# Sixteen projection units as whole 128-row products into one PSUM bank, rounded straight from PSUM, and a first pair of rows loaded on an earlier schedule

## The chip, the cores and the metric

The kernel runs on one core of a Trainium2 chip. The time is the device time of one execution in microseconds (us). Below, PE is TensorE, ACT is ScalarE, DVE is VectorE, POOL is GpSimd, and SP is the engine that issues nearly all DMAs. PEld is the profile's name for PE's weight loads.

## What is computed

A gate mixes an attention layer and a Fourier mixing layer, both on the same x of 2048 rows by 512 columns:

```python
qkv = (x @ wqkv) -> q, k, v, 32 heads of 16      # S = 2048, D = 512
a = softmax(q k^T / 4) v @ wo
b = dft_seq_re @ (x @ dft_hid_re^T) - dft_seq_im @ (x @ dft_hid_im^T)
g = sigmoid((x * gate_w).sum(-1))
out = g * a + (1 - g) * b
```

## The kernel before

**Number format.** Most matrix products run on fp32 values rounded to TensorE's float32r format. Each operand is kept as two parts, a rounded one (`hi`) and what is left of it (`lo`, rounded too), and one product is summed from three: hi·hi, lo·hi and hi·lo. `split` (line 351) makes the parts: ACT copies into float32r (line 352), and DVE or POOL subtracts (line 353).

**Halves.** `halves_of` (line 200, product at 204) cuts each 128-row contraction into two products of 64 rows. They lie in the upper and the lower half of the array and write to two PSUM banks, so that the result is the sum of the two banks. The scans, which run between other products later on, also use rows 0 to 47 and 64 to 111.

**Units and slots.** `project_t` (line 480) makes one unit of the q and k projections: 128 columns of the weights against 512 rows of x, over four blocks `d` of the contraction and three part products each, so twelve steps. A step is called a slot here. `products` (line 343) issues them and calls `beside` (line 307) after each. `beside` counts the slots and runs what is due: `after(n, f, ...)` (line 282) registers a piece of work for n slots later. So the order of every engine's instructions follows from slot numbers, while the times on the chip follow from the waits. Engines work through their own instructions strictly in that order.

**The end of a unit before.** ACT copies bank 0 to `tx` (line 489). Five slots later DVE adds bank 1 (line 492). Nine slots after the unit ACT rounds the sum to `hi` (tile `eh`, three buffers), then POOL subtracts to `lo` (tile `el`, four buffers). The two parts go to DRAM (`q_d`, `k_d`) by DMAs due 14 and 20 slots after the unit (line 499). Work registered by `after` carries line 297 in the profile. An `eh` buffer is written again three units later, so the store of three units before has to have landed.

**The first sixteen units.** They run before any scan (`pace[0]` is None). Here they are called u0 to u15: u0 (q), u1 (k) and u2 (q) take x block c=0; u3 and u4 take c=1, u5 and u6 c=2, u7 and u8 c=3 (q then k each time); u9 to u15 are further q units. Between u7 and u8 stand the gate sums (line 573), 16 plain fp32 products of 128 rows by 32 columns, and in the middle of u8 four transposes of their result. u0, u2, u4 and u6 write to the `s1` banks, all others to the two `wide` tiles in turn, named `xy`. x is split while this goes on (line 567): the four blocks `d` of x block c are split at slots 24c-6+4d, ACT and DVE doing one instruction each.

**The rows of the first pair.** The scans search the maxima of the scores, and need rows of q and k of two heads in SBUF. `load_scan_beside` (line 299) reads those of the first pair from `q_d` and `k_d` with eight DMAs on SP (line 116), four for each head; it is due 22 slots after u8, and the eight are 7 slots apart. 84 slots after u8, at the end of u15, `scan_at(PACE)` starts the scans: one every 3.9 slots, each with a product for either head (line 154) and a maximum on DVE (line 156). The first one stands behind the third slot of u16.

**SP.** SP issues its DMAs in order. They share eight semaphores in turn, so a DMA is only issued when the one eight before it has landed; a wait on `DMAHW0` to `DMAHW7` in the order's rows is such a wait, or one for data.

Of the kernel before, what the change touches and what calls it, by code (L numbers as in the profile page):

```python
# [10 lines left out]
F32 = mybir.dt.float32  # L11
F32R = mybir.dt.float32r
# [6 lines left out]
P = 128  # L19
# [6 lines left out]
ND = D // P  # L26
# [40 lines left out]
def build(tc, xT, wqkv, wo, wrT, wiT, cr, ci, ct, gate, out):  # L67
    nc = tc.nc
    with ExitStack() as ctx:
# [130 lines left out]
        def halves_of(ps, lhs, rhs, first, last):  # L200

            for j in range(2):
                r = slice(64 * j, 64 * j + 64)
                nc.tensor.matmul(ps[j], lhs[r], rhs[r], start=first, stop=last)  # L204
# [6 lines left out]
        def wide(i, name):  # L211
            return psf.tile([P, 2, 512], F32, tag=f"wide{i}", name=name)
# [56 lines left out]
        pace = [None, 0.0]  # L269
        with ExitStack() as pf:  # L270
# [6 lines left out]
            def xy():  # L277
                turns[0] += 1
                ps = wide(turns[0] % 2, "xy")
                return ps[:, 0, :], ps[:, 1, :]  # L280

            def after(n, f, *args):

                count[0] += 1
                due.append((slots[0] + n, count[0], f, args))
# [13 lines left out]
            def load_scan_beside(p):  # L299
                scanned[p], loads = row_loads(p, nc.sync, kf_d if p else k_d)  # L300
                for n, load in enumerate(loads):
                    after(7 * n, load)

            def scan_at(spacing):
                pace[0] = spacing
# [34 lines left out]
                    scan_folded(n, 1, *beds)  # L340
                    return n

            def products(ps, parts):
                n = 0
                for lhs, rhs in parts:
                    for a, b in ((0, 0), (0, 1), (1, 0)):
                        halves_of(ps, lhs[a], rhs[b], n == 0, n == 3 * len(parts) - 1)
                        n += 1
                        beside()

# [15 lines left out]
            for ph, plain, pair in ((0, range(NB - 2), (NB - 2, NB - 1)), (1, range(2, NB), (0, 1))):  # L366
                split_up = [(ph, t, u) for half in range(2) for t in pair for u in (2 * half, 2 * half + 1)]
                whole = [(ph, t, u) for t in plain for u in range(NU)]
# [29 lines left out]
            with ExitStack() as px:  # L398
                wb = px.enter_context(tc.tile_pool(name="wb", bufs=1))
                ep = px.enter_context(tc.tile_pool(name="ep", bufs=2))  # L400
# [78 lines left out]

                def project_t(w, dst, f, c, ps=None):  # L480
                    ps = ps or xy()
                    products(ps, [([w[i][d][:, f * P:(f + 1) * P] for i in range(2)], xs[d, c])
                                  for d in range(ND)])
                    tx = ep.tile([P, 512], F32, tag="tx", name="tx", bufs=1)
                    folded = dst is k_d
                    s = ep.tile([P, 512], F32, tag="ty", name="s", bufs=3)
                    hi = ep.tile([P, 512], F32R, tag="eh", name="eh", bufs=3)
                    lo = ep.tile([P, 512], F32R, tag="el", name="el", bufs=4)
                    nc.scalar.copy(tx, ps[0])
                    on_vector = pace[0] in (None, SUMS)  # L490
                    if on_vector:
                        after(5, nc.vector.tensor_add, s, ps[1], tx)
                    else:
                        after(3, nc.scalar.copy, s, ps[1])
                        after(5, nc.gpsimd.tensor_add, s, s, tx)
                    late = 0 if on_vector else 6

                    def store(i, v):
                        nc.sync.dma_start(dst[f][:, i, c * 512:(c + 1) * 512], v.bitcast(F32))
                        if folded and f and c % 2:  # L500
                            nc.sync.dma_start(kf_d[f][:, i, c * 512:(c + 1) * 512], v.bitcast(F32))

                    if folded and f == 1:
                        difference(f, c, s)
                    if folded and f == 2:
                        after(10, nc.sync.dma_start, ks_d[f][:, c * 512:(c + 1) * 512], s)
                    after(9 + late, nc.scalar.copy, hi, s)
                    after(10 + late + late // 3, nc.gpsimd.tensor_sub, lo, s, hi.bitcast(F32))
                    after(14 + late, store, 0, hi)
                    after(20 + late, store, 1, lo)  # L510
# [73 lines left out]
                for n, (w, dst, f, c) in enumerate(order):  # L584
                    lead = s1() if n in (0, 2, 4, 6) else None
                    project_t(w, dst, f, c, lead and (lead[:, 0, :], lead[:, 1, :]))
                    if n == 7:
                        gate_sums()
                after(22, load_scan_beside, 0)
                after(84, scan_at, PACE)  # L590
                for f, c in [(2, 0), (3, 0)] + [(f, c) for f in range(1, ND) for c in range(1, NC)]:
                    project_t(wq, q_d, f, c)
# [59 lines left out]
            with ExitStack() as py:  # L652
# [36 lines left out]
                for n, (ph, t, u) in enumerate(coef):  # L689
# [12 lines left out]
                    hi, lo = ready.pop(n)  # L702
# [47 lines left out]
        with ExitStack() as pa:  # L750
# [143 lines left out]
            parts = []  # L894
# [299 lines left out]
            for step in range(NP * PERIODS):  # L1194
                p, i = step // PERIODS, step % PERIODS
# [133 lines left out]
```

## Time and profile before

| | |
|---|---|
| time, median of 3 runs | 1715.07 us (1714.08 to 1715.12) |
| the profiled execution | 1715.43 us, its span 1713.6 us |
| granted TensorE clock | 0.999 |
| instructions | 36496 |
| HBM read, written | 158.34 MB, 81.01 MB |

The profile is of one execution. Times in it count from the span's start; the 1.8 us between span and time lie around the program. A row of the timeline gives the start in us, the length in us, engine, line, operation, tiles, how many instructions were merged into it, and in brackets how long the engine was idle before it and what ended that. Matmul records are longer than the time that a product takes up, since products overlap in the array: what counts is the distance between starts.

### The profile page before, as it was taken

What the parts mean: (1) busy time and instruction counts of PE and PEld (TensorE: products, weight loads), DVE (VectorE), ACT (ScalarE), POOL (GpSimd) and SP (SyncE); (2) the same over time, 40 slices, a digit from 0 to 9 for tenths busy, and PEclk for the clock granted to TensorE, in tenths of its full rate; (3) what the DMA queues carried; (4) which work ended last, traced back from release to release, by engine and by line L of the source; (5) the groups of instructions that cost most, each with busy time, mean ns of one, the idle gap of its engine ahead of it and who ended that gap; (6) DMA issues with size and microseconds to landing.
All of it is one profiled execution on the core that took longest, in us unless ns stands there. A gap on an engine that the chain in (4) does not pass through costs nothing.

```text
span 1713.6 us, 36496 instructions
## 1 busy us (share of the span) xinstructions
PE 1700.1 (99%) x13560; PEld 1033.2 (60%) x13560; DVE 1189.9 (69%) x2179; ACT 1496.6 (87%) x2472; POOL 764.1 (45%) x909
## 2 busy tenths in 40 slices
PE   9999999999999999999999999999999999999998
PEld 6888888989888895333333333333345555555554
DVE  5798888889899996666666676666642455654343
ACT  6447889888888888999999999999998988888876
POOL 3583335755555762433535455353422333334222
PEclk9999999999999999999999999999999999999999
DMA  7783457533337665356544445453436465576733
GB/s 255 237 286 86 149 153 224 155 107 108 112 106 199 176 132 109 89 128 149 138 112 113 121 114 135 100 124 85 95 73 144 133 148 148 141 160 168 192 93 126
DMA packets 148962, 240.97 MB, mean 141 GB/s; under 512 B 50048, under 2 KB 60784, under 8 KB 142192
## 3 DMA queue, kind: packets, MB, share of 16 engines
q1 hardware_dynamic: 133520, 217.27, 47.5%
q0 software_dynamic: 14688, 20.33, 5.0%
q8 instruction: 106, 1.74, 0.5%
q10 hardware_dynamic: 576, 1.05, 0.2%
q14 instruction: 72, 0.59, 0.1%
HBM read 158.34 MB, written 81.01 MB: 140 GB/s over the span
## 4 chain that ended last, share of the span: by engine, by line
PE 95%; issue 1%; POOL 1%; DMA 1%; DVE 1%; ACT 0%; SPq 0%; DVEq 0%; POOLq 0%; ACTq 0%
PE pvb L775 29%; PE xy L204 24%; PE s L229 19%; PE s L173 9%; PE s L204 9%; PE s L154 5%; POOL el L297 1%; DMA raws<-wqkv 0%; DMA qs<-q_d 0%; DVE y L890 0%; DVE fold L179 0%; ACT fold L177 0%; DVE s L297 0%; SPq L543 0%; SPq L542 0%
## 5 line engine op out<-in xcount | busy, mean ns | idle before, releaser
L253 ACT ACTIVATE eb<-s 128x1024 f32<-128x1024 f32 x512 | 582.0, 1137 | 59.6 <-PE s L229 59.5
L261 ACT ACTIVATE e<-s 128x512 f32<-128x512 f32 x1022 | 612.3, 715 | 0.0
L156 DVE TENSOR_REDUCE mx<-s 128x2 f32<-128x1024 f32 x380 | 461.0, 1224 | 197.5 <-PE s L154 197.3
L775 PE MATMUL pvb<-eb,va 128*17 128x512 f32 x2052 | 514.6, 597 | 0.0
L775 PE MATMUL pvb<-e,va 128*17 128x512 f32 x2044 | 513.6, 597 | 0.0
L179 DVE CUSTOM_DVE_ANT_0 fold<-s,fold 128x512 f32<-128x512 f32 x644 | 433.2, 690 | 57.3 <-PE s L173 29.9
L177 ACT ACTIVATE fold<-s 128x512 f32<-128x512 f32 x644 | 381.4, 603 | 76.8 <-PE s L173 58.9
L229 PEld LDWEIGHTS s<-qs,ks 50*128 50x128 f32 x2048 | 215.4, 185 | 361.4 <-ACT eb L253 269.4
L229 PE MATMUL s<-qs,ks 50*128 50x512 f32 x2048 | 424.3, 435 | 0.0
L204 PE MATMUL xy<-b,c 64*128 64x512 f32 x2448 | 394.7, 392 | 0.2 <-ACT c L352 0.2
L173 PE MATMUL s<-ks,qs 48*128 48x512 f32 x1288 | 306.1, 403 | 1.7 <-DVE mx L179 0.9
L204 PEld LDWEIGHTS xy<-b,c 64*128 64x128 f32 x2448 | 285.7, 187 | 16.9 <-issue 1.0
L173 PEld LDWEIGHTS s<-ks,qs 48*128 48x128 f32 x1288 | 167.1, 184 | 40.4 <-DVE mx L179 10.7
L775 PEld LDWEIGHTS pvb<-eb,va 128*17 128x17 f32 x2052 | 70.0, 96 | 188.1 <-issue 178.5
L154 PE MATMUL s<-ks,qs 48*128 48x512 f32 x760 | 158.5, 394 | 0.9 <-DMA qs<-q_d 0.9
L204 PE MATMUL s<-b,b 64*128 64x512 f32 x1050 | 136.3, 391 | 0.0
L794 POOL DMA_DIRECT2D r_d<-lc x31 | 18.0, 580 | 260.6 <-DVE lc L793 212.9
L204 PE MATMUL xy<-w,b 64*128 64x512 f32 x768 | 114.8, 392 | 0.0
L204 PEld LDWEIGHTS s<-b,b 64*128 64x128 f32 x1050 | 100.3, 185 | 23.4 <-issue 1.0
L787 POOL DMA_DIRECT2D lc<-ob x124 | 63.0, 515 | 114.4 <-DVE ob L784 109.6
L384 POOL TENSOR_TENSOR c<-craw,c 128x512 fp32r<-128x512 f32 x84 | 110.2, 1312 | 6.7
L796 POOL DMA_DIRECT2D rb<-r_d x124 | 60.5, 494 | 110.6 <-DMA r_d<-lc 104.7
(148 smaller groups left out, 1567.3 us busy)
## 6 DMA issues: line engine op xcount, KB each, us to landing
qs<-q_d SPq DMA_DIRECT2D x68, 256.0 KB
craw<-cr SPq DMA_DIRECT2D x60, 256.0 KB
craw<-ct SPq DMA_DIRECT2D x48, 256.0 KB
ks<-k_d SPq DMA_DIRECT2D x46, 256.0 KB
kept_None<-sum SPq DMA_DIRECT2D x40, 256.0 KB
craw<-kept_None SPq DMA_DIRECT2D x40, 256.0 KB
qs<-q_d SPq DMA_DIRECT2D x68, 128.0 KB
craw<-ci SPq DMA_DIRECT2D x32, 256.0 KB
```

Of the source, the lines that this page charges most:

```text
L154: nc.tensor.matmul(ps[:, j, :], qs[b:b + 48, qb * P:(qb + 1) * P], ks[b:b + 48, c * 512:(c + 1) * 512], start=True, stop=True)
L156: nc.vector.tensor_reduce(mx[p][:, :, qb, c], ps, axis=AX.X, op=ALU.max)
L173: nc.tensor.matmul(ps, qs[b:b + 48, qb * P:(qb + 1) * P], ks[b:b + 48, c * 512:(c + 1) * 512], start=True, stop=True)
L177: nc.scalar.activation(fold[j], ps, AF.Relu)
L179: nc.vector.tensor_tensor_reduce(out=fold[j], in0=ps, in1=fold[j], scale=1.0, scalar=-3.0e38, op0=ALU.add, op1=ALU.max, accum_out=mx[p][:, ...
L204: nc.tensor.matmul(ps[j], lhs[r], rhs[r], start=first, stop=last)
L229: nc.tensor.matmul(pss[j], ks[b:b + 50, kb * P:(kb + 1) * P], qs[b:b + 50, q0:q0 + 512], start=True, stop=True)
L253: nc.scalar.activation(e, ps, AF.Exp, scale=SCALE)
L261: nc.scalar.activation(e[j], pss[j], AF.Exp, scale=SCALE)
L384: sub(lo, raw, hi.bitcast(F32))
L775: nc.tensor.matmul(pvb[r:r + VC, :], va[:, kb, 2 * p + j, :], es[c][j], start=kb == 0, stop=kb == NB - 1, tile_position=(0, r))
L787: nc.gpsimd.dma_start(lc[32 * n:32 * n + 32, :], ob[r + DH:r + VC, :].rearrange("p (s e) -> p s e", e=16))
```

## The change

Three things change, all in the first 60 us of the program.

1. In the first sixteen units `products` issues one product of 128 rows into one bank in place of the two of 64 rows. That is 192 products and weight loads in place of 384.
2. At the end of such a unit ACT rounds the bank straight to `hi`, as the unit's last product ends. Four slots later DVE subtracts `hi` from the bank to give `lo`. The stores are due 5 and 9 slots after the unit. The copy to `tx`, the addition, and POOL's subtraction are gone for these units.
3. The first pair's eight loads are due from 14 slots after u8, 6 slots apart.

```diff
             def load_scan_beside(p):
                 scanned[p], loads = row_loads(p, nc.sync, kf_d if p else k_d)
                 for n, load in enumerate(loads):
-                    after(7 * n, load)
+                    after((7 if p else 6) * n, load)
...
-            def products(ps, parts):
+            def products(ps, parts, whole=False):
                 n = 0
                 for lhs, rhs in parts:
                     for a, b in ((0, 0), (0, 1), (1, 0)):
-                        halves_of(ps, lhs[a], rhs[b], n == 0, n == 3 * len(parts) - 1)
+                        if whole:
+                            nc.tensor.matmul(ps[0], lhs[a], rhs[b], start=n == 0, stop=n == 3 * len(parts) - 1)
+                        else:
+                            halves_of(ps, lhs[a], rhs[b], n == 0, n == 3 * len(parts) - 1)
                         n += 1
                         beside()
...
                 def project_t(w, dst, f, c, ps=None):
                     ps = ps or xy()
+                    whole = pace[0] is None
                     products(ps, [([w[i][d][:, f * P:(f + 1) * P] for i in range(2)], xs[d, c])
-                                  for d in range(ND)])
+                                  for d in range(ND)], whole)
+                    if whole:
+                        hi = ep.tile([P, 512], F32R, tag="eh", name="eh", bufs=3)
+                        lo = ep.tile([P, 512], F32R, tag="el", name="el", bufs=4)
+                        nc.scalar.copy(hi, ps[0])
+                        after(4, nc.vector.tensor_sub, lo, ps[0], hi.bitcast(F32))
+                        for i, (wait, v) in enumerate(((5, hi), (9, lo))):
+                            after(wait, nc.sync.dma_start, dst[f][:, i, c * 512:(c + 1) * 512], v.bitcast(F32))
+                        return
...
-                after(22, load_scan_beside, 0)
+                after(14, load_scan_beside, 0)
```

In the rows below the numbers at the ends of names tell buffers apart, and the brackets name the semaphores that an instruction waits for. In the new program's rows the lines are those of the new file.

ACT, before, from u3's copy to u5's. `tx_463`, `tx_502` and `tx_541` are u3, u4 and u5; `eh_465` is u3's `hi`; `b20_223` and `b22_225` are the hi parts of x block c=2, d=2 and d=3.

```order
L489 COPY tx_463<-xy_425 128x512 [waits PE_49,Activation_49]
L352 CAST b20_223<-raws_243 128x512 [waits DMAHW0_49]
L352 CAST b22_225<-raws_244 128x512 [waits DMAHW1_49]
L297 CAST eh_465<-s_464 128x512 [waits DMAHW1_49,DVE_49]
L489 COPY tx_502<-s1_468 128x512 [waits PE_49,Activation_49]
L352 CAST b24_227<-raws_241 128x512 [waits DMAHW2_49]
L297 CAST eh_504<-s_503 128x512 [waits DMAHW3_49,DVE_49]
L352 CAST b26_229<-raws_242 128x512
L489 COPY tx_541<-xy_507 128x512 [waits PE_49,Activation_49]
```

The same stretch of ACT in the new program; `eh_405`, `eh_428` and `eh_451` are the `hi` of u3, u4 and u5.

```order
L491 CAST eh_405<-xy_381 128x512 [waits DMAHW1_49,DVE_49,PE_49]
L355 CAST b20_223<-raws_243 128x512 [waits DMAHW0_49]
L355 CAST b22_225<-raws_244 128x512
L491 CAST eh_428<-s1_408 128x512 [waits DVE_49,DMAHW3_49,PE_49,Activation_49]
L355 CAST b24_227<-raws_241 128x512 [waits DMAHW2_49]
L355 CAST b26_229<-raws_242 128x512
L491 CAST eh_451<-xy_431 128x512 [waits DMAHW5_49,DVE_49,PE_49]
```

u3's rounding, which waits for the landing of u0's `hi` store (`DMAHW1`), stood behind the splits of x block c=2, d=2 and d=3; now it stands ahead of them.

DVE, new program, the same stretch: the splits' `lo` parts and the units' `el`.

```order
L356 TENSOR_TENSOR b21_224<-raws_243,b20_223 128x512 [waits DMAHW0_49,Activation_49]
L297 TENSOR_TENSOR el_406<-xy_381,eh_405 128x512
L356 TENSOR_TENSOR b23_226<-raws_244,b22_225 128x512 [waits DMAHW1_49,Activation_49]
L297 TENSOR_TENSOR el_429<-s1_408,eh_428 128x512 [waits DMAHW2_49,Activation_49]
L356 TENSOR_TENSOR b25_228<-raws_241,b24_227 128x512 [waits Activation_49]
```

The places are those of before; what stood there was the addition of the two banks, and is now the subtraction that gives `lo`.

SP, before, from the second store of u10 to the last of the first pair's loads; `eh_798` and `el_799` are u11's stores, `eh_836` and `el_837` u12's.

```order
L499 DMA q_d3_80<-el_760 128x512 [waits Pool_49]
L116 DMA ks_750<-k_d0_81 32x1x2048 [waits DMAHW3_49]
L499 DMA q_d1_78<-eh_798 128x512 [waits DMAHW4_49,Activation_49]
L499 DMA q_d1_78<-el_799 128x512 [waits DMAHW5_49,Pool_49]
L116 DMA qs_749<-q_d0_77 32x2048 [waits DMAHW6_49]
L499 DMA q_d1_78<-eh_836 128x512 [waits DMAHW7_49,Activation_49]
L116 DMA ks_750<-k_d0_81 16x2048 [waits DMAHW0_49]
L499 DMA q_d1_78<-el_837 128x512 [waits DMAHW1_49,Pool_49]
L116 DMA qs_749<-q_d0_77 16x2048 [waits DMAHW2_49]
```

The same stretch of SP in the new program, with u11's `eh_611` and `el_612` and u12's `eh_634`.

```order
L297 DMA q_d3_80<-el_589 128x512 [waits DVE_49]
L116 DMA ks_570<-k_d0_81 32x1x2048 [waits DMAHW3_49]
L297 DMA q_d1_78<-eh_611 128x512 [waits DMAHW4_49,Activation_49]
L116 DMA qs_569<-q_d0_77 32x2048 [waits DMAHW5_49]
L297 DMA q_d1_78<-el_612 128x512 [waits DMAHW6_49,DVE_49]
L116 DMA ks_570<-k_d0_81 16x2048 [waits DMAHW7_49]
L297 DMA q_d1_78<-eh_634 128x512 [waits DMAHW0_49,Activation_49]
L116 DMA qs_569<-q_d0_77 16x2048 [waits DMAHW1_49]
```

Each of the last three loads moved past one store. The first five keep their places among the stores, and the last now stands behind u12's `hi` store instead of its `lo` store.

DVE, new program, where the scans begin: `el_677` and `el_696` are u14 and u15, `mx_706` takes the scans' maxima.

```order
L297 TENSOR_TENSOR el_677<-xy_660,eh_676 128x512 [waits DMAHW2_49,Activation_49]
L156 TENSOR_REDUCE mx_706<-s1_705 128x2 [waits PE_49]
L297 TENSOR_TENSOR el_696<-xy_679,eh_695 128x512 [waits DMAHW6_49,Activation_49]
L156 TENSOR_REDUCE mx_706<-s1_720 128x2 [waits PE_49]
L156 TENSOR_REDUCE mx_706<-s1_733 128x2 [waits PE_49]
```

u15's subtraction stands between the first two maxima. Before, u15's banks were summed on POOL, and no other DVE work stood between the first maxima.

## The prediction

> **What bounds the kernel now.** I read the page's busy times and chain first, then the timeline of the first 62 us engine by engine, since the change touches nothing later.
>
> ```profile
> PE 1700.1 (99%) x13560; PEld 1033.2 (60%) x13560; DVE 1189.9 (69%) x2179; ACT 1496.6 (87%) x2472; POOL 764.1 (45%) x909
> PE 95%; issue 1%; POOL 1%; DMA 1%; DVE 1%; ACT 0%; SPq 0%; DVEq 0%; POOLq 0%; ACTq 0%
> ```
>
> PE's own work is 95% of the chain that ends last, and PE runs in a fixed order. So the change is worth what it moves the point at which the scans run, and PE carries that shift to the end. I take the product of the first scan's second half, at 58.80 here, as that point. PE's timeline up to it:
>
> ```profile
> 21.61 2.68 PEld L204 LDWEIGHTS xy<-b,w 64*128 64x128 f32 x24
> 21.83 2.88 PE L204 MATMUL xy<-b,w 64*128 64x512 f32 x24
> 24.55 2.88 PE L204 MATMUL s<-b,c 64*128 64x512 f32 x24
> 29.87 0.30 PEld L204 LDWEIGHTS xy<-b,w 64*128 64x128 f32 x4 [0.56 <-DVE b L353]
> 29.87 0.73 PE L204 MATMUL xy<-b,w 64*128 64x512 f32 x4
> 34.10 1.66 PE L204 MATMUL xy<-b,c 64*128 64x512 f32 x12
> 35.70 0.42 PEld L297 LDWEIGHTS s<-ident,zr 128*128 128x128 f32 x4 [0.37 <-issue]
> 35.70 0.66 PE L297 MATMUL s<-ident,zr 128*128 128x128 f32 x4
> 36.28 1.64 PE L204 MATMUL xy<-b,c 64*128 64x512 f32 x12
> 37.76 19.88 PE L204 MATMUL xy<-b,w 64*128 64x512 f32 x174
> 57.48 0.40 PE L154 MATMUL s<-ks,qs 48*128 48x512 f32 x1
> 58.77 0.18 PEld L154 LDWEIGHTS s<-ks,qs 48*128 48x128 f32 x1 [1.33 <-DMA ks<-k_d]
> 58.80 0.46 PE L154 MATMUL s<-ks,qs 48*128 48x512 f32 x1 [0.92 <-DMA qs<-q_d]
> ```
>
> Rows two and three are u5 and u6. They start 2.72 us apart, which for 12 slots is 0.2267 us a slot. Of these 2.72 us the weight loader is busy for 2.68. The two rows at 29.87 are the eleventh and twelfth slot of u7, after a wait for a split. u8 begins at 34.10, with the gate sums ahead of it and four transposes in its middle; the long row begins with u9. The last three show the scan's first half at 57.48 and its second half waiting for rows until 58.80, 1.3 us.
>
> **The whole product's pace.** No row shows a float32r product of 128 rows by 512 columns, so I bound it. It has half the weight loads, so the loader no longer binds (12 x 2.68/24 = 1.34 us a unit), if loads still run under products. In u5's rows they do: 2.68 us of loads lie within 2.72 us, and each half of the array is also streaming. The streaming is measured by the gate sums:
>
> ```profile
> 31.42 0.13 PEld L573 LDWEIGHTS s<-raws,gw 128*32 128x32 f32 x4 [0.30 <-issue]
> 31.85 0.13 PEld L573 LDWEIGHTS s<-raws,gw 128*32 128x32 f32 x4 [0.30 <-issue]
> L573 PE MATMUL s<-raws,gw 128*32 128x512 f32 x32 | 3.6, 595 | 0.0
> L204 PE MATMUL xy<-b,w 64*128 64x512 f32 x336 | 42.4, 389 | 0.1
> ```
>
> Their groups of four records, side by side, start 0.43 us apart, and one is 0.595 long, so 0.165 us of a record is tail. A half product's record of 0.389 less this tail is 0.22 us. **I take 0.22 us a slot.** The program has 16 gate products and the trace 32 records, so each fp32 product passes twice; if each pass also reads its 512 columns twice, a single pass takes 0.214, the lower end. The upper end is load and product in turn, 0.22 + 0.112 (2.68/24) = 0.332.
>
> [...]
>
> **What becomes late first.** With `hi` rounded at a unit's end, its buffer is needed 9 slots sooner. The stores cannot land sooner, because they queue behind the loads of x and the weights:
>
> ```profile
> 12.90 0.62 ACT L297 CAST eh<-s 128x512 fp32r<-128x512 f32 x1 [0.24 <-DVE s L297]
> 15.22 0.34 SPq L554 DMA_DIRECT2D ones_d<-ones  x1
> 15.87 0.34 SPq L499 DMA_DIRECT2D q_d<-eh  x1
> 20.08 1.14 ACT L352 CAST b<-raws 128x512 fp32r<-128x512 f32 x2
> 23.53 0.62 ACT L297 CAST eh<-s 128x512 fp32r<-128x512 f32 x1 [2.31 <-DMA q_d<-eh]
> 25.47 0.62 ACT L297 CAST eh<-s 128x512 fp32r<-128x512 f32 x1 [0.31 <-DVE s L297]
> 22.23 0.68 DVE L353 TENSOR_TENSOR b<-raws,b 128x512 fp32r<-128x512 f32 x1
> ```
>
> u0's `hi` store is issued at 15.87, and u3's rounding waits for its landing until 23.53. u0's `hi` is ready at 13.52 already; the store only comes to its turn on SP behind `ones_d`, whose data were there from the start. An earlier `hi` doesn't move it, so 23.53 stands. But before, the casts of x block c=2, d=2 and d=3 (20.08) were done ahead of that wait; in the new order they are behind it. They then run 24.15 to 25.4 (0.62 each). DVE follows: `b21_224` to 25.55, u3's `el` to 26.25, `b23_226` to 26.95 (0.69 each). u5 needs `b20_223` at its seventh slot (23.2 at the old pace) and `b23_226` at its eleventh (24.1). It waits until 27.0; the slot after such a wait takes 0.34 (in u7: 0.73 for two slots, less a record of 0.39). So u6 starts at 27.0 + 0.34 + 0.22 = 27.56, against 24.55: **+3.0 us**. A faster start of u1 to u4 (4 x 12 x 0.0067) is swallowed by this wait. u4's rounding at 25.4 finds its buffer free, as it did at 25.47.
>
> **From there to the scan.**
> - u7 starts at 27.56 + 12 x 0.22 = 30.20. u5's rounding (from 27.75) and two casts end on ACT at 29.6, and DVE's three subtractions from 29.0 on at 31.1; u7 needs the last at its eleventh slot, 32.40, so the old wait goes. From that slot to u8 were 34.10 - 29.87 = 4.23 us, now 4.11, as the slot behind takes 0.22: u8 at 36.51, +2.4.
> - u8: six slots to 37.73, 0.22 to the first transpose, four transposes at 0.11 (their loads take 0.42), six slots: u9 at 39.71 against 37.76, +1.95. I leave out the gaps around the transposes (36.28 is 0.58 behind the first of them, not 0.44, and the halves' rows on both sides hold more than five slots of 0.2267), since products and transposes now both use the whole array.
> - u9 to u15: 84 x 0.0067 = -0.56, u16 at 58.19 against 56.80.
> - The scan's products stand 0.68 behind u16's start; with 0.1 for the change from whole array to halves, 58.97.
>
> Do the rows arrive by then?
>
> ```profile
> 40.39 0.32 SPq L499 DMA_DIRECT2D k_d<-eh  x1
> 42.53 0.65 SPq L116 DMA_DIRECT2D ks<-k_d  x1
> 51.56 1.30 POOL el L297
> 52.87 0.33 SPq L499
> 53.25 5.46 DMA qs<-q_d
> ```
>
> The first load waits for u8's `hi` store, issued at 40.39, to land: 42.53. The new order rounds that part when u8's last record ends, at 39.88, and its store can go at 40.6, the first load at 42.7; **the shorter slot numbers do not move it**. The last load stood behind u12's `lo` from POOL (52.87), and landed at 58.71. Now it stands behind u12's `hi`: u13 starts at 39.71 + 4 x 2.64 = 50.27, u12's last record ends at 50.44, `hi` at 51.1, and the load can be issued at 51.5, 1.7 us sooner. From first load to last landing were 16.2 us on busy queues; with one store of 0.65 less, 42.7 + 15.5 = 58.2. That is before 58.97, so the 1.3 us of waiting go, with 0.8 to spare. The point moves from 58.80 to 58.97: **+0.2 us**.
>
> **DVE behind it.**
>
> ```profile
> 58.21 1.28 POOL L297 TENSOR_TENSOR s<-s,tx 128x512 f32<-128x512 f32 x1 [0.47 <-ACT s L297]
> 59.30 7.06 DVE L156 TENSOR_REDUCE mx<-s 128x2 f32<-128x1024 f32 x6 [3.58 <-PE s L154]
> 59.00:70.00 11.00, 11.00 (x96) 9.90 (x96) 10.70 (x10) 4.26 (x9) 5.55 (x5) 1.00 0.26 96
> 70.00:80.00 10.00, 10.00 (x90) 8.75 (x88) 9.56 (x9) 4.42 (x9) 7.67 (x6) 1.00 0.75 248
> ```
>
> From 59.30 on DVE reduces without a gap, 1.18 us a scan, about PE's pace; u15's addition was POOL's. Now u15's subtraction, 0.69, stands between the first two maxima. With two banks a scan waits only when DVE is over half a scan behind, and between 70 and 80 DVE (fourth figure) has 0.44 us to spare. Between 0 and 0.69 I take **+0.2 us**, nearer the end at which spare time absorbs it.
>
> The rest brings nothing. POOL loses 15 subtractions of 1.3 us (the row at 51.56), and ACT the copies to `tx`, but neither ended a wait of PE in the first 110 us; these are all of them behind the first transposes:
>
> ```profile
> PE s L204 <- ACT w L352: 1.1, 2, 0.8
> PE s L154 <- DMA qs<-q_d: 0.9, 1, 0.9
> PE xy L204 <- ACT c L352: 0.2, 1, 0.2
> ```
>
> The work taken away was hidden under PE's products, and what stands in its place is too, but for the two places above.
>
> **Sum.** u5's wait +3.0; u7's wait -0.4 and the gaps around the transposes -0.4; pace behind u5 -0.8 (120 slots x 0.0067); rows' wait -1.3; switch and DVE +0.3, rounded to **+0.4 us**. The profiled execution took 1715.43, its span and 1.83 around it, and would become 1715.8. It lay 0.36 above the median, so against the median I forecast **1715.5 us**.
>
> **Rivals.**
> 1. *The pace stays at 0.2267*, a fixed cost per slot rather than the loader. For it: no row shows a slot without its two loads. Against: 2.68 of 2.72. +0.8: 1716.3.
> 2. *u5 does not wait*, because the stores land by 21 us. For it: the wait at 23.53 rests on how fast the queues took the loads in this one execution. Against: the store's place on SP is the same. u5 then starts at 21.5 (48 slots at 0.0067 sooner) and u7 at 26.8, 3.4 sooner than above: 1712.1; at 0.214 in all 192 slots another 1.1 less, 1711.0.
> 3. *Slower: a weight load does not run under a product on the same rows.* Then a slot is 0.332. u5 starts at 21.83 + 48 x 0.105 = 26.9, its wait is swallowed, u8 starts at 42.4, u9 at 47.1, the scan at 75.8: +17, 1732. It decides from 0.245 a slot, where 120 x 0.025 adds the 3 us that make 0.2%. Against it stand the four transposes at 35.70: four loads of the whole array's weights at 0.105 and four streams of 128 columns (at the gate sums' rate 0.43/512 x 128 = 0.107) in turn would take 0.85 us and a tail, and they took 0.66 with it. They are plain fp32 of 128 columns, so float32r at 512 is not shown. [...]
> 4. *128 rows of float32r stream at the gate sums' rate*, 0.43 a slot: by the same steps the scan comes at 93, +34, 1750. For it: every 128-row product in the trace has that rate. Against: those are fp32.
>
> **How the numbers follow.** Forecast 0.60, rival 1 0.13, rival 2 0.10, rival 3 0.12, rival 4 0.04, another 0.01. The range takes the first three, 0.83: from rival 2's lower end, 1711.0, to rival 1 with DVE's full 0.69 and 1 us for rows that land late, 1717.8. A difference of 0.2%, 3.4 us, is about what a measurement can tell from no change. Faster by that is only rival 2's lower end and a little of the forecast: 0.07. Slower is rivals 3 and 4 and a little more: 0.17. The rest, 0.76, is within.
>
> **What would show it.** In the new profile: starts of u9 to u15 2.64 apart; a wait of ACT on `q_d<-eh` until 23.5 with the casts of x behind it, and PE waiting for DVE's `b` near 25 to 27; u9 near 39.7; no PE wait on rows at the first scan, near 59.0. Starts 2.72 or 4 us apart tell rivals 1 and 3; u6 near 24.1 tells rival 2. The forecast is wrong if a slot is above 0.245 or the time moves behind 60 us.

## The result, and the profile after

The changed kernel takes **1716.9 us** (median of 21 runs, 1715.33 to 1721.24) against 1714.09 for the kernel before on the same chip (21 runs, 1712.85 to 1715.19): a ratio of 1.0018, with a 95% interval of 1.0011 to 1.0025. It is slower by a little, inside the forecast's range, but by 2.8 us where +0.4 was forecast. The profiled execution took 1717.26 us, its span 1715.3, at a granted clock of 0.999.

PE's timeline of the changed kernel, for the same stretch as before (start, length, engine and line, tiles, count, idle time before it):

```profile
21.83 1.52 PE L348 MATMUL xy<-b,w 128*128 128x512 f32 x6
23.71 0.50 PE L348 MATMUL xy<-b,w 128*128 128x512 f32 x1 [0.35 <-ACT b L355]
24.43 0.96 PE L348 MATMUL xy<-b,w 128*128 128x512 f32 x3 [0.22 <-DVE b L356]
25.63 0.73 PE L348 MATMUL xy<-b,w 128*128 128x512 f32 x2 [0.24 <-DVE b L356]
26.21 2.89 PE L348 MATMUL s<-b,c 128*128 128x512 f32 x12
28.94 2.88 PE L348 MATMUL xy<-b,w 128*128 128x512 f32 x12
35.32 1.66 PE L348 MATMUL xy<-b,c 128*128 128x512 f32 x6
36.81 0.60 PE L297 MATMUL s<-ident,zr 128*128 128x128 f32 x4
37.17 1.63 PE L348 MATMUL xy<-b,c 128*128 128x512 f32 x6
38.63 19.20 PE L348 MATMUL xy<-b,w 128*128 128x512 f32 x84
57.77 0.96 PE L204 MATMUL xy<-b,w 64*128 64x512 f32 x6
58.57 0.40 PE L154 MATMUL s<-ks,qs 48*128 48x512 f32 x2
```

u5 (21.83) now waits for splits, as forecast, and u6 starts at 26.21, against 24.55. u6 takes 2.73 until u7, and u9 at 38.63 to u16 at 57.77 is 19.14 for 84 slots, 0.228 each (before: 0.2267): **the slot kept its old length**. The scan no longer waits for rows: its two halves start together at 58.57, where the second half stood at 58.80 before.

The wait behind u5 is ACT's, for the landing of u0's `hi` store, with the casts of x behind it:

```profile
22.55 0.59 ACT L491 CAST eh<-xy 128x512 fp32r<-128x512 f32 x1 [4.33 <-DMA q_d<-eh]
23.03 1.14 ACT L355 CAST b<-raws 128x512 fp32r<-128x512 f32 x2
24.07 0.59 ACT L491 CAST eh<-s 128x512 fp32r<-128x512 f32 x1
```

So the front is no later than before, in this execution. Four places tell where the time went. They are the first maximum of the scans (DVE, L156), the first and the last `eb` of the attention (ACT, L253), and the end of the span. The first maximum before stood at 59.30; the two rows of `eb` before:

```profile
658.49 1.03 ACT L253 ACTIVATE eb<-s 128x1024 f32<-128x1024 f32 x1 [3.35 <-PE s L229]
1695.91 1.02 ACT L253 ACTIVATE eb<-s 128x1024 f32<-128x1024 f32 x1 [0.47 <-PE s L229]
```

The three after:

```profile
59.04 1.23 DVE L156 TENSOR_REDUCE mx<-s 128x2 f32<-128x1024 f32 x1 [2.58 <-PE s L154]
657.47 1.03 ACT L253 ACTIVATE eb<-s 128x1024 f32<-128x1024 f32 x1 [3.35 <-PE s L229]
1697.30 1.02 ACT L253 ACTIVATE eb<-s 128x1024 f32<-128x1024 f32 x1 [0.48 <-PE s L229]
```

| us | before | after | difference |
|---|---|---|---|
| to the first maximum | 59.30 | 59.04 | -0.26 |
| to the first `eb` | 599.19 | 598.43 | -0.76 |
| **first to last `eb`** | 1037.42 | 1039.83 | **+2.41** |
| last `eb` to the end (tail) | 17.74 | 18.03 | +0.29 |

The loss lies a thousand microseconds behind the change, in code that it does not touch. (The second row scattered between 598.2 and 599.5 over all kernels below, of both kinds, so I draw nothing from it. The table compares two executions, which lie 1.8 us apart; the medians lie 2.8 apart.) Followed `eb` by `eb`, the 2.41 come mainly in four steps: +0.43 near 872, +0.46 near 994, +0.24 near 1116, and +1.3 between 1675 and 1690.

**The step at 1682.** The engines' waits from 1655 to 1700 (engine, tile and line, what was waited for: us, times, longest), before:

```profile
DVE y L890 <- PE s L204: 24.7, 9, 3.2
POOL rb L796 <- DMA r_d<-lc: 1.4, 1, 1.4
```

And after:

```profile
DVE y L902 <- PE s L204: 26.1, 9, 4.5
POOL rb L808 <- DMA r_d<-lc: 3.2, 1, 3.2
PEld s L204 <- DMA b<-o_d: 1.5, 4, 0.5
PE s L204 <- DMA b<-o_d: 0.4, 2, 0.2
```

A transfer of 8 KB, the reciprocals of the softmax sums, landed 1.8 us later, with it the quotients `o_d`, and PE waited for `b<-o_d`, which it did not before. The DMA queues from 1668.7 to 1672.2 say what was different. Before:

```profile
q0 software_dynamic: 61, 0.04, 4.5%
r_d<-lc POOLq DMA_DIRECT2D x1, 8.0 KB, 1.7
```

After (packets, MB, share of 16 engines; the last row's 3.5 is us from issue to landing):

```profile
q8 instruction: 1, 0.02, 2.4%
q0 software_dynamic: 32, 0.01, 2.0%
r_d<-lc POOLq DMA_DIRECT2D x1, 8.0 KB, 3.5
```

One packet of queue q8 lies beside the transfer: 16 KB of kind *instruction*. Its 2.4% of 16 engines and 3.5 us is 1.3 us on one engine.

**The step at 872.** POOL and DVE, before:

```profile
869.96 1.27 POOL L797 TENSOR_TENSOR ob<-ob,rb 128x512 f32<-128x512 f32 x1 [2.15 <-DMA rb<-r_d]
871.05 0.22 DVE L196 CAST chi<-mt 128x32 fp32r<-128x32 f32 x1
871.79 1.23 DVE L156 TENSOR_REDUCE mx<-s 128x2 f32<-128x1024 f32 x1 [0.52 <-PE s L154]
```

And after, where all but the landing was 1.0 us earlier:

```profile
869.96 1.28 POOL L809 TENSOR_TENSOR ob<-ob,rb 128x512 f32<-128x512 f32 x1 [3.16 <-DMA rb<-r_d]
870.02 1.27 DVE L196 CAST chi<-mt 128x32 fp32r<-128x32 f32 x1
871.20 1.21 DVE L156 TENSOR_REDUCE mx<-s 128x2 f32<-128x1024 f32 x1
```

POOL waited 3.16 us for `rb<-r_d`, not 2.15; a 16 KB instruction packet of 1.15 us lay inside that wait. So POOL's product began 0.06 us ahead of DVE's small cast, and the cast lasted until that product's end (870.02 + 1.27 = 871.29; 869.96 + 1.28 = 871.24) instead of 0.22. DVE's maximum comes late, and PE's loads wait 0.6 us for it between 869 and 880, which they did not before. The two profiles have twelve of these casts (`chi<-mt`) on DVE: the ten that began while an instruction of POOL ran all ended 0.03 to 0.04 us after it, and the two others took 0.18 us. What ties the cast to POOL's instruction no run shows.

The steps near 994 and 1116 are of the same kind: POOL waited 3.14 and 3.00 us for `rb<-r_d` with a packet inside (before: 1.70 and 1.60, none inside), and the cast took 1.27 and 1.11 (before: 0.51 and 0.37). The late landing is not enough by itself. In whole_from_u11, a kernel below, it came near 870 and 991 too (waits of 3.31 and 3.26, a packet in each), but there the cast began 0.13 and 0.08 us ahead of POOL's product and took 0.17, and no step followed.

### The profile page after: what moved, and what is told of

It reads as the page before. It is cut to its first block, busy times and chain, and to the rows that moved or that the text cites. A ratio compares the mean times of both kernels' runs of the same rounds, so it can differ in the third digit from the quotient of the medians.

```text
span 1715.3 us, 36057 instructions
## 1 busy us (share of the span) xinstructions
PE 1702.4 (99%) x13368; PEld 1028.6 (60%) x13368; DVE 1183.5 (69%) x2180; ACT 1487.9 (87%) x2455; POOL 742.2 (43%) x892
## 4 chain that ended last, share of the span: by engine, by line
PE 96%; DMA 2%; DVE 1%; issue 1%; SPq 0%; POOL 0%; ACT 0%; DVEq 0%; POOLq 0%; ACTq 0%
PE pvb L787 28%; PE xy L204 25%; PE s L229 19%; PE s L173 9%; PE s L204 8%; PE s L154 5%; PE xy L348 1%; DMA q_d<-eh 0%; DMA raws<-wqkv 0%; DMA raws<-xT 0%; PE s L585 0%; DMA r_d<-lc 0%; DVE y L902 0%; PE s L348 0%; DMA b<-o_d 0%
## 5 line engine op out<-in xcount | busy, mean ns | idle before, releaser
L253 ACT ACTIVATE eb<-s 128x1024 f32<-128x1024 f32 x512 | 574.8, 1123 | 61.3 <-PE s L229 60.8
L261 ACT ACTIVATE e<-s 128x512 f32<-128x512 f32 x1022 | 605.0, 701 | 0.0
L156 DVE TENSOR_REDUCE mx<-s 128x2 f32<-128x1024 f32 x380 | 460.5, 1223 | 192.8 <-PE s L154 192.5
L204 PE MATMUL xy<-b,c 64*128 64x512 f32 x2400 | 388.6, 392 | 0.0
L204 PEld LDWEIGHTS xy<-b,c 64*128 64x128 f32 x2400 | 280.8, 187 | 15.2
L386 POOL CAST c<-craw 128x512 fp32r<-128x512 f32 x84 | 52.4, 624 | 119.4 <-PE xy L204 116.5
## 6 DMA issues: line engine op xcount, KB each, us to landing
qs<-q_d SPq DMA_DIRECT2D x68, 256.0 KB
craw<-cr SPq DMA_DIRECT2D x60, 256.0 KB
craw<-ct SPq DMA_DIRECT2D x48, 256.0 KB
ks<-k_d SPq DMA_DIRECT2D x46, 256.0 KB
kept_None<-sum SPq DMA_DIRECT2D x40, 256.0 KB
craw<-kept_None SPq DMA_DIRECT2D x40, 256.0 KB
craw<-ci SPq DMA_DIRECT2D x32, 256.0 KB
```

The costliest lines, as they stand in the source:

```text
L156: nc.vector.tensor_reduce(mx[p][:, :, qb, c], ps, axis=AX.X, op=ALU.max)
L253: nc.scalar.activation(e, ps, AF.Exp, scale=SCALE)
L261: nc.scalar.activation(e[j], pss[j], AF.Exp, scale=SCALE)
```

## The experiments

The packets' rhythm points to a cause. The page of before has 13,560 weight loads, and its trace 106 packets of 16 KB on q8; behind 600 us one comes every 127 weight loads on average (singly, 72 to 182). The change takes away 192 of them in the first 58 us, one and a half packets, so the later packets should lie about half a distance off: near the last sums packets start at 1659.8 and 1676.6 before, and at 1669.9 after. Below, the *shift* is the number of weight loads added or taken away, modulo 128 (an extra semaphore instruction of PE counts half). The 128 is an estimate from the traces: before's has 27,273 instructions of PE, 13,560 loads, as many products and 153 others (150 of them semaphore instructions), and from its first packet to its last 255.8 of them start per packet (256.0 in the changed kernel's); at two instructions a product, load and stream, that is 128 loads. That the packets are PE's is read from this rhythm, and from their number: 107 with 13,624 weight loads (before_pad), 105 with 13,368 (the changed kernel).

The first four kernels were made before I had seen this. Their theories: W, that u5's wait is carried to the end; C, that the granted clock stays low for longer at the start; L, that something collides behind 60 us.

**rows_only**: the kernel before, with the earlier rows alone.

```diff
-                    after(7 * n, load)
+                    after((7 if p else 6) * n, load)
...
-                after(22, load_scan_beside, 0)
+                after(14, load_scan_beside, 0)
```

> The kernel before with only the first pair's loads on the new slots (14 slots after u8, 6 apart); products and rounding as before. Theory W (the wait of u5 for late roundings costs 1.7 to 3 us and PE carries it to the end): no such wait arises here, and the last load still stands behind a part that POOL makes, so the time is the same or up to 0.7 us shorter, ratio 0.9995 to 1.0002. Theory C (in part of the runs the granted clock is low for longer at the start, because whole products come too sparsely there): ratio 1.000, spread of the times as for the kernel before. Theory L (the loss arises behind 60 us, where the same program meets other collisions of DVE, POOL and DMAs): a shift of under 1 us in the rows changes the later part by up to 2 us either way.

1714.3 us (11 runs), ratio 1.0001 (0.9992 to 1.001). First to last `eb` 1037.37, tail 17.75. The earlier rows neither gain nor lose anything that can be measured. In its profile half of the wait is left, though: the second half of the first scan starts 0.66 us behind the first half, where it was 1.32, and the first maximum is at 58.70, 0.6 sooner. The interval is too wide to tell 0.6 us from nothing.

**late_round**: the changed kernel with the old slots for rounding and stores.

```diff
-                        nc.scalar.copy(hi, ps[0])
-                        after(4, nc.vector.tensor_sub, lo, ps[0], hi.bitcast(F32))
-                        for i, (wait, v) in enumerate(((5, hi), (9, lo))):
+                        after(9, nc.scalar.copy, hi, ps[0])
+                        after(10, nc.vector.tensor_sub, lo, ps[0], hi.bitcast(F32))
+                        for i, (wait, v) in enumerate(((14, hi), (20, lo))):
```

> The changed kernel, but each of the sixteen units is rounded nine slots after its end and subtracted at ten, with the stores due at 14 and 20, as before the change; products stay whole. So u3's rounding stands behind the casts of x again. Theory W: u5's wait goes, u6 starts near 24.5, u7's old wait of 0.4 us may return: 1.5 to 2.5 us less than the changed kernel, ratio 0.9990 to 1.0003. Theory C: as the changed kernel, 1.0018, with its spread and some runs at a granted clock of 0.998. Theory L: the scan point comes earlier, but the part behind it is as long as in the changed kernel's profile (1656 us from the first maximum to the end, against 1654), ratio 1.0005 to 1.0015.

1716.05 us, ratio 1.0009 (1.0 to 1.0017). PE's row of u5 is whole again:

```profile
21.60 2.88 PE L348 MATMUL xy<-b,w 128*128 128x512 f32 x12
24.32 2.88 PE L348 MATMUL s<-b,c 128*128 128x512 f32 x12
```

u6 starts 1.9 us sooner and the first maximum is at 57.58, 1.46 sooner than in the changed kernel, but first to last `eb` still takes 1039.02 and the tail 18.03. W holds for the front, but the ratio that it expected (0.9990 to 1.0003) did not come; L's (1.0005 to 1.0015) did. The loss behind the front is another thing.

**whole_from_u6**: whole units from u6 on.

```diff
-                    whole = pace[0] is None
+                    whole = pace[0] is None and slots[0] >= 72
```

> The changed kernel, but u0 to u5 are made as before (two halves, sum of two banks, late rounding); u6 to u15 are whole and rounded at their end. Theory W: no wait in u5, rows early enough: ratio 0.9988 to 1.0000. Theory C: the sparse start is that of the kernel before, so all runs show a clock of 0.999 and the spread of before; ratio 0.999 to 1.000. Theory L: ratio 1.0005 to 1.0015, with the loss behind 60 us.

1713.26 us (1712.63 to 1713.54), ratio 0.9993 (0.9984 to 1.0002). First to last `eb` 1037.23, tail 17.75: the later loss is gone. The ratio is the one that W and C expected, not L's.

**warm36**: the changed kernel with `NWARM` 36 in place of 20, that is 16 more warm-up transposes.

> The changed kernel with 36 warming transposes at the start instead of 20, which keep PE busy until 6 to 8 us, while the first operands still land. Theory W: as the changed kernel, ratio 1.0012 to 1.0022. Theory C: the spread shrinks to that of the kernel before, no run under 0.999, ratio 1.0005 or less. Theory L: as the changed kernel within 1 us.

1718.21 us, ratio 1.0023 (1.0014 to 1.0032). First maximum at 61.76, first to last `eb` 1038.82. Seven of its ten runs had a mean granted clock of 0.998, and its profile shows one way to that. The columns are the window, its length, the five engines' busy times, the granted clock, DMA share and GB/s:

```profile
23.60:27.00 3.40, 1.74 (x5) 0.95 (x6) 2.22 (x4) 3.15 (x6) 0.00 (x0) 1.00 0.59 224
27.00:30.40 3.40, 3.40 (x9) 2.63 (x9) 2.96 (x6) 1.93 (x4) 0.00 (x0) 0.50 0.80 301
30.40:33.80 3.40, 3.40 (x16) 2.76 (x16) 2.04 (x5) 1.20 (x3) 0.00 (x0) 1.00 0.36 134
```

For 3.4 us the clock was granted by half, behind u5's waits, and u6 took 4.1 us in place of 2.72. So such a window exists in single executions, but C's own numbers for this kernel (no run under 0.999, 1.0005 or less) did not come. Of the changed kernel's 21 runs 6 had 0.998 or 0.997, and all but those had a median of 1716.6. So this adds at most 0.3 us to the median and is not the main loss. At most, because a mean of 0.998 does not prove an early window: the profiles of whole_to_u10 and whole_from_u8, below, have that mean with a clock of one half only at the end (from 1707.7 and 1709.3).

The next four test **theory F, the phase of the instruction packets**, against A, that the early units being whole is what counts.

**whole_to_u10** (shift -4) has the line `whole = pace[0] is None and slots[0] < 131`.

> The changed kernel, with units u0 to u10 whole and u11 to u15 as halves again. Theory F (the phase of TensorE's instruction packets): the profile lists a queue q8, kind instruction, with packets of 16 KB, one per some 129 weight loads of TensorE (13,713 TensorE records and 106 packets before). In the kernels whose later part is long, a 16 KB packet lies inside the few small transfers of the softmax sums (rb<-r_d and r_d<-lc) some ten times and each then takes 3.3 to 3.9 us in place of 2.1; in the quick kernels once or twice. The change takes 192 weight loads away, one and a half packets, which moves the packets by half their distance; here 132 are taken away, within 4 of one whole packet. F expects first eb to last eb at 1037.4 (1037.1 to 1037.8) and a tail of 17.75, with u6 late as in the changed kernel (26.2 +- 0.6), and a median near 1714.2 (1713.4 to 1715.0). Theory A (the early units being whole is what counts, by the other addresses of the rounding tiles that go with it): 1038.8 to 1039.8, a tail of 18.03, and a median of 1716 to 1717.

1715.33 us, ratio 1.0007 (0.9998 to 1.0016). First to last `eb` 1037.33, though u0 to u5 are whole and u6 is as late as in the changed kernel (26.43). Here F's number came, A's did not. The median is 0.3 us over F's range (up to 1715.0), and the tail, 18.14, is not F's 17.75; more on it below.

**whole_from_u11** (shift +68) has `slots[0] >= 131`.

> The changed kernel, with only units u11 to u15 whole and u0 to u10 as before; the rounding tiles lie at the addresses of before. 60 weight loads fewer than before, within 4 of half a packet (64). Theory F: the early units run as before (no late u6: 24.6 to 25.0) and yet first eb to last eb is 1038.8 to 1039.8 and the tail 18.03; median 1715.3 to 1716.8. Theory A: 1037.3 and 17.75 as in the kernel with u6 to u15 whole, median 1713.2 to 1714.3.

1716.47 us, ratio 1.0013 (1.0004 to 1.0023). The front is like before's (u6 at 24.47), the early units are halves, and yet first to last `eb` takes 1039.18, as F expected. The tail is 17.77, not F's 18.03. The waits near the end are those of the changed kernel:

```profile
POOL rb L808 <- DMA r_d<-lc: 3.4, 1, 3.4
PEld s L204 <- DMA b<-o_d: 1.7, 4, 0.7
```

**after_pad** (shift 0) is the changed kernel, with other warm-up transposes.

```diff
-                for n in range(NWARM):
+                for n in range(8):
                     nc.tensor.transpose(warm[:, n % 2, 0:P], ident, ident)
+                for n in range(76):
+                    nc.tensor.transpose(warm[0:32, n % 2, 0:32], ident[0:32, 0:32], ident[0:32, 0:32])
```

> The changed kernel with nothing changed in the units: of the 20 warm-up transposes 12 are replaced by 76 of 32 x 32, so that TensorE has 64 weight loads more and stands at 128 fewer than before, exactly one packet. Theory F: first eb to last eb 1037.4 (1037.1 to 1037.8), tail 17.75, with the early wait of u5 kept; median near 1714.2 if the warm-up ends when it did, plus what it ends later. Theory A: 1038.8 to 1039.8 and 18.03, median 1716 to 1717.

1716.34 us, ratio 1.0014 (1.0005 to 1.0022). The warm-up ended about 2 us late (u0 at 7.42, against 5.54), so the first maximum is at 60.62, and the time did not come down to 1714.2. F's 1714.2 with this delay is 1716.1 and A expected 1716 to 1717, so the median does not tell them apart. But first to last `eb` is 1037.35: **64 weight loads of 32 x 32 ahead of the first unit took 2.5 us out of the attention a thousand microseconds on**. From 1668 to 1672.2 no instruction packet lies beside the transfer:

```profile
q0 software_dynamic: 64, 0.01, 2.2%
r_d<-lc POOLq DMA_DIRECT2D x1, 8.0 KB, 1.7
```

**late_to_u10** (shift -3) joins the later rounding with whole units to u10.

> The kernel with the later rounding (copy after 9 slots, difference after 10, stores after 14 and 20), units u0 to u10 whole, 131 weight loads fewer than before. The later rounding alone had its first maximum at 57.58 but first eb to last eb 1039.02 and a median of 1716.05. Theory F: 1037.4 and a tail of 17.75 here, the first maximum near 57.6, so a median of 1713.0 to 1714.4. Theory A: 1039.0, 18.03 and 1716.

1714.28 us (1713.43 to 1714.76, and one execution of 7072.91 of which there is no trace), ratio 0.9998 (0.9989 to 1.0007). First to last `eb` 1037.49, first maximum 57.51, as F expected, though the tail is 17.97 and not 17.75; 1.8 us less than late_round, with u11 to u15 halves again and the other shift.

**before_pad** (shift +64) is the converse: the kernel before, none of the change.

```diff
-                for n in range(NWARM):
+                for n in range(2):
                     nc.tensor.transpose(warm[:, n % 2, 0:P], ident, ident)
+                for n in range(82):
+                    nc.tensor.transpose(warm[0:32, n % 2, 0:32], ident[0:32, 0:32], ident[0:32, 0:32])
```

> The kernel before with none of the change: of the 20 warm-up transposes 18 are replaced by 82 of 32 x 32, so that TensorE has 64 weight loads more, half a packet, in the warm-up alone; the 82 at 54 ns end about a microsecond later than the 18. Theory F (the phase of the instruction packets): first eb to last eb grows from 1037.4 to 1038.8 to 1039.8, with 16 KB packets inside three or more of the transfers rb<-r_d and r_d<-lc that took 2.1 and 1.4; median 1715.8 to 1717.8. Theory A (whole units are needed for the loss): 1037.4 there, and a median of 1714.2 to 1715.4, later by the warm-up alone.

1716.16 us, ratio 1.001 (1.0001 to 1.0018): slower, by the amount that F expected. Its profile does not show it, though: it is the fastest of the 11 runs (1713.41; the others 1714.78 to 1717.24), with first to last `eb` 1037.31. All of POOL's waits for `rb<-r_d` in the kernel before, in us and times:

```profile
  DMA rb<-r_d: 60.5, 31
```

The same in before_pad:

```profile
  DMA rb<-r_d: 67.6, 31
```

So the packets did move into the transfers (the changed kernel has 69.0). But at the last sums the packet started 0.91 us behind the end of the issue of `r_d<-lc` and missed it:

```profile
POOL rb L798 <- DMA r_d<-lc: 1.4, 1, 1.4
```

In whole_from_u11 it started 0.87 us behind, and the wait was 3.4. Expected of the profile and not seen, then; seen in the median, whose place in the program no profile shows.

**whole_from_u8** (shift +32, `slots[0] >= 96`) and **whole_from_u3** (shift -28, `slots[0] >= 36`) stand between.

> The changed kernel with units u8 to u15 whole and u0 to u7 as before: 96 weight loads fewer, so 32 ahead of a whole packet, a quarter of the distance and the middle between the quick kernels (0 to 8, 124 to 128) and the slow ones (64 to 80). Theory F says no more than that the packets lie about 4 us later than in the quick kernels: first eb to last eb between 1037.2 and 1039.5, by how many of the small transfers are hit (nearest rows: none more than 2 hit, 1037.4; eight hit, 1039.2). Theory A: 1037.3, median 1713.2 to 1714.3, since the early units are halves.

1714.79 us, ratio 1.0006 (0.9997 to 1.0015); first to last `eb` 1037.93. Its tail is 19.34: there a 16 KB packet of 1.3 us lies among the last stores of the output, which end 1.6 us later than before. But this execution took 1716.58, the second longest of the 11, so this tail is not that of the median. A's 1713.2 to 1714.3 did not come, and F had given no time.

> The changed kernel with units u3 to u15 whole: 156 weight loads fewer, 28 short of a whole number of packets, so the packets lie some 4 us earlier than in the quick kernels. Theory F: between 1037.2 and 1039.0, 1037.5 likeliest, since the packet ahead of the last sums then lies ahead of the transfer r_d<-lc. u3 and u4 whole put u3's rounding ahead of the casts, so u6 late by about 1.5 as in the changed kernel (25.6 to 26.8). Median 1713.8 to 1716.

1717.65 us, ratio 1.0021 (1.0012 to 1.003), over the expected range. First to last `eb` is 1038.2, within F's bounds but not its likeliest; u6 came at 27.13, later than expected, and 5 of the 11 runs had a mean clock of 0.998; in the profile, which is that of the fastest of the 11, the clock is halved from 11.06 to 14.47, in u1.

**late_from_u6** joins the later rounding with whole_from_u6 (shift +8).

> The best kernel so far, u6 to u15 whole (1713.26), with the later rounding and stores (after 9, 10, 14 and 20 slots) in those units: 8 from a whole packet. Theory F: first eb to last eb 1037.3, a median of 1712.6 to 1713.6, that is 0.6 to 1.6 below the kernel before: faster than both by a little. If the later rounding gains its microsecond only where the early units are whole, no difference to 1713.26.

1714.88 us, ratio 1.0004 (0.9995 to 1.0012). First to last `eb` is 1037.25, as expected, but the time is not: it is 1.6 us over whole_from_u6. In the profiled execution u1 started at 11.94 (before: 10.79; whole_from_u6: 11.03), on weights that landed later; whether that holds for the median is open. So whole_from_u6 stays the fastest of all, 0.8 to 0.9 us below the kernel before, with an interval that still holds 1.

All profiles together, one execution each. "Hit" counts those of POOL's waits for `rb<-r_d` (31 in a kernel) in which a 16 KB packet ran at some time between the issue of the transfer and the end of the wait:

| kernel | shift | hit | last `r_d<-lc` | wait of PE's loads for `b<-o_d` | first to last `eb` |
|---|---|---|---|---|---|
| before | 0 | 1 | 1.4 | none | 1037.42 |
| rows_only | 0 | 2 | 1.4 | none | 1037.37 |
| after_pad | 0 | 1 | 1.4 | none | 1037.35 |
| whole_from_u6 | +8 | 2 | 1.4 | none | 1037.23 |
| late_from_u6 | +8 | 2 | 1.4 | none | 1037.25 |
| whole_to_u10 | -4 | 2 | 1.4 | none | 1037.33 |
| late_to_u10 | -3 | 1 | 1.4 | none | 1037.49 |
| whole_from_u3 | -28 | 6 | 1.4 | 0.9 | 1038.20 |
| whole_from_u8 | +32 | 7 | 1.4 | 0.6 | 1037.93 |
| warm36 | -48 | 15 | 1.4 | 1.3 | 1038.82 |
| late_round | -63 | 12 | 3.0 | 1.4 | 1039.02 |
| **after** | 64 | 10 | 3.2 | 1.5 | 1039.83 |
| whole_from_u11 | +68 | 9 | 3.4 | 1.7 | 1039.18 |
| before_pad | 64 | 11 | 1.4 | none | 1037.31 |

Seven kernels within 8 of a whole packet lie within 0.26 us of each other, whatever their early units are; the others are 0.4 to 2.6 longer, but for before_pad's one execution. Over the whole table the transfer that ended such a wait took 2.81 us from issue to landing in the 81 hits (the median), and 1.98 in the 353 other waits.

The step near the last sums is the largest wherever there is a loss: +1.25 in late_round, +1.54 in whole_from_u11, +1.11 in warm36. Where `r_d<-lc` was missed, a packet lay beside another transfer of the same sums: in warm36 `lc<-ob` took up to 3.05 us in place of 1.5, in whole_from_u8 `rb<-r_d` up to 3.47 in place of 2.0, and in whole_from_u3 the second `b<-o_d` was issued 1.57 us behind the first, in place of 0.7.

The tail does not follow the shift of PE's packets: F's number for it failed in all four kernels for which it was given (whole_to_u10, whole_from_u11, after_pad, late_to_u10), and A's came within 0.11. It is 17.74 to 17.77 in the kernels whose early units are halves, but for whole_from_u8, and 17.97 to 18.14 in all that have u3 whole. In whole_to_u10 the last output store took 1.04 us to issue on ACT, not 0.46. An 8 KB instruction packet of queue q14, at 1.8 us ahead of that issue, is my suspect; that was not tested, and the 0.29 us stay open.

## Why the prediction was right within its range and wrong in size

- **The pace of the whole products** (the term -0.8): wrong. A slot is still 0.228 us from u9 to u16, so rival 1's pace is the true one, and what sets it is open: the loads, half as many, were busy for 15.58 us of these 19.14, against 15.77 of 19.04 before, and not for the half that the forecast took. The forecast's 0.22 came from subtracting a tail that it took from fp32 records, and from rounding: 0.389 less 0.165 is 0.224, with which the term would have been -0.3. A slot of 0.214, the lower end taken there, did not appear either. Rivals 3 and 4 are out: 0.228 is far from 0.332 and 0.43, and the products' records fill all of the 19.14 us, so the 15.58 us of loads of the whole array lie under products on the same rows.
- **u5's wait** (+3.0): the mechanism was right, the size was 1.66. The store landed so that ACT went on at 22.55, not 23.53, though it was issued at 16.15, later than the 15.87 of before; why it took less time is open. From there ACT's instructions followed each other at about 0.5 us, not 0.62, and the splits with them. The order and the waits were those described. late_round shows that it is this wait, since u6 is 1.9 us earlier without it. In the median its price was about 1 us (1716.9 to 1716.05, and whole_to_u10's 1715.33 to late_to_u10's 1714.28).
- **u7's wait and the gaps at the transposes** (-0.4 each): right. u7's wait is gone, and the lag of 1.66 at u6 shrinks to 0.87 at u9, a gain of 0.79 (0.44 up to u8, 0.35 behind it). One step of the working is off by 0.1: six slots of 0.22 from 36.51 end at 37.83, not 37.73.
- **The rows' wait** (-1.3): right, it is gone. What it is worth by itself is not shown: in rows_only only half of it went, and the times (1714.3 against 1714.2) don't resolve that.
- **Switch and DVE** (+0.3): the switch cost 0.12 (57.77 to 58.57, where it was 56.80 to 57.48). u15's subtraction put the second maximum 1.74 us behind the first (1.17 before), but 60 maxima on only 0.07 us of that is left.
- **The point**: +0.2 forecast; -0.2 at the second half of the first scan, and -0.26 at the first maximum. Two errors in opposite directions, 0.9 in the pace and 1.3 in u5's wait, met in a sum that looked exact: that is luck.
- **The range.** That 1716.9 lies in it is luck as well. Its upper end, 1717.8, counts from the 1715.07 of three runs; from the 1714.09 of 21 runs the same steps end at 1716.8. And no term of it stood for a loss behind 60 us.
- **"The change touches nothing later"**: this step failed, and it is the missing term of the sum, +2.4 us in the attention and +0.3 in the tail. The list of what would prove the forecast wrong has it, "the time moves behind 60 us", without a mechanism or a price. In its place the runs showed: 192 weight loads fewer on PE moved its later instruction packets (near the last sums from 1659.8 and 1676.6 to 1669.9); these land inside small transfers that something waits for (waits of 3.2 us in place of 1.4 for the last `r_d<-lc`, and of 3.16 in place of 2.15 for an `rb<-r_d`). That the packet is the cause rests on the timing at the four steps, on the 81 hits against the 353 other waits, and on kernels in which 60 to 64 weight loads, here or there, brought the loss in (whole_from_u11; before_pad by its median) or took it away (after_pad, whole_to_u10). Only the 2.4 us are explained in this way; the 0.3 of the tail stay open.

## What to carry to other kernels

Here 192 weight loads fewer on PE moved its later instruction packets by about half their distance, and 2.4 us were lost in steps 800 to 1600 us on; in a kernel tuned to a microsecond, look for queue q8 inside the waits for small transfers, far behind the change, before explaining a loss near it. Compare variants at equal instruction counts modulo a packet, or pad them, or the comparison also measures the phase, here 2.5 us (after_pad). And the pace that the rows showed, 0.2267, was a better guess for the new shape, which took 0.228, than the 0.22 from a difference of two record lengths.

## What the runs showed of the hardware that was not expected

- By their rhythm and number, the 16 KB packets of kind *instruction* on queue q8 carry TensorE's instructions, one for about 127 weight loads. One packet took 0.88 to 1.82 us before and 0.88 to 2.08 in the changed kernel, and waits for a small transfer with one inside were 1.0 to 2.0 us longer (`rb<-r_d` 3.16 in place of 2.15; `r_d<-lc` 3.2, and 3.4 in whole_from_u11, in place of 1.4).
- A packet that started 0.87 us behind the end of the issue of `r_d<-lc` went with a wait of 3.4 us (whole_from_u11), one 0.91 us behind it with 1.4 (before_pad), in one execution each; that the 0.04 us decided it is not shown.
- A float32r product of 128 rows by 512 columns started every 0.228 us (84 of them from u9 to u16), about as two of 64 rows side by side did before (0.2267).
- The granted clock fell to one half for 3.4 us early in the program, from 27.0 to 30.4 in warm36, behind u5's waits, and from 11.1 to 14.5 in whole_from_u3; the unit at that place took 1.3 to 1.4 us more.
